# The kv products of six batches: pairs of 128 by 64 column tiles in place of whole-array products of a head pair

## The chip, the cores and the metric

The kernel runs on one core of a Trainium2 chip. The metric is the device time of one execution, in microseconds. Executions of one kernel differ by a few tenths of a per cent, and a change is timed against the kernel before on the same chip.

## The reference

An attention of a linear kind is followed by a two-layer network with a Swish. There are 8 batches, 8 heads, 576 rows and 64 columns per head.

```python
q_s = softmax(q, axis=-1)            # over the 64 columns
k_s = softmax(k, axis=2)             # over the 576 rows
kv  = einsum('bhsd,bhse->bhde', k_s, v)     # 64 x 64 per head: "the kv products"
x   = einsum('bhsd,bhde->bhse', q_s, kv)    # then heads side by side: 4608 x 512
h   = x @ w_in                       # 4608 x 2048
out = (h / (1 + exp(-beta * h))) @ w_out    # 4608 x 512
```

The two large products with `w_in` and `w_out` are most of the arithmetic. The kv products are a small part, and they are what is changed.

## The kernel before

Per batch and head pair, the kernel sums `exp(k)` transposed times `v`. The 576 rows are four slices of 128 and a tail of 64 (padded with zeros to 128), so there are five products per head pair. The values have a column of constants next to them, `D1 = 65` columns per head, so that column 64 gives the softmax denominator.

```python
# batches 2 to 7 (b >= NW); n = 2 head pairs per call
def kv_mm(b, jj, n=2, tag="att"):
    t = ps.tile([P, n, 2 * D1], F32, ...)
    for jl in range(n):
        j = n * jj + jl
        # ... batches 0 and 1: nine products of 65 columns, zero-padded weights ...
        for i in range(R):                     # four slices of 128 rows
            nc.tensor.matmul(
                t[:, jl, :],                                        # 128 x 130
                ek[b][:, i, 2*j : 2*j+2, :].rearrange(...),         # weights 128 x 128: two heads
                va[b][:, i, 2*j : 2*j+2, :].rearrange(...),         # 130 columns: two heads
                start=(i == 0), stop=False)
        nc.tensor.matmul(t[:, jl, :], ekt[...], vt[...], start=False, stop=True)   # the tail
```

Half of each 128 by 130 result is never used: the rows of one head meet the values of the other. `kv_norm` takes the two useful quarters and divides them. The calls are spread among the steps `u` of the large products of the batch before:

```python
def side(c, u):                        # o = 2 for the first batch, else 0
    ...
    if u in (8 + o, 10 + o) and not tail:
        kv_mm(b, (u - 8 - o) // 2)     # "a group": ten products
        kv_norm(b, (u - 8 - o) // 2)
...
for j in range(...):
    mm_a(c, j)          # four 512-column products with w_in
    mm_b(c, j - LAG)    # four 512-column products with w_out
    side(c, j)
```

So each group of ten products stands between 512-column products, and there are 12 groups (two in each of six batches).

The softmax here doesn't subtract the row's maximum and nothing guards it: scores larger than these inputs give would overflow.

Of the kernel before, what the change touches and what calls it, by code (L numbers as in the profile page):

```python
# [10 lines left out]
F32 = mybir.dt.float32  # L11
# [6 lines left out]
def kernel(  # L18
# [10 lines left out]
    nc = tc.nc  # L29
# [6 lines left out]
    NJ = FF // P  # L36
# [5 lines left out]
    NW = 2  # L42
    D1 = D + 1
    LAG = 2
    NCH = B + 1

    const = ctx.enter_context(tc.tile_pool(name="const", bufs=1))
    stage = ctx.enter_context(tc.tile_pool(name="stage", bufs=1))
# [26 lines left out]
    def load_q(b, parts=1):  # L75
        t = stage.tile([P, H, R * D], F32, tag="q_st", bufs=2, name=f"q_st{b}")
        src = q[b, :, 0:MAIN, :].rearrange("h (p i) d -> p h (i d)", i=R)
        n = H // parts
        for s in range(parts):
            nc.sync.dma_start(t[:, s * n : (s + 1) * n, :], src[:, s * n : (s + 1) * n, :])  # L80
        q_st[b] = t
# [12 lines left out]
    def load_kv(d, src, b, tag, parts=1):  # L94
        t = stage.tile([P, H * (R + 1) * D], F32, tag=tag, bufs=2, name=f"{tag}{b}")
        if b < NW:
            d[b] = t[:, 0 : HP * RW * D].rearrange("p (j r) -> p j r", j=HP)
            sv = src[b].rearrange("(j e) (p i) d -> (e p) j (i d)", e=2, i=RW)
            n = HP // parts
            for s in range(parts):  # L100
                nc.sync.dma_start(d[b][:, s * n : (s + 1) * n, :], sv[:, s * n : (s + 1) * n, :])
        else:
            d[b] = t[:].rearrange("p (h r) -> p h r", h=H)
            nc.sync.dma_start(
                d[b][:, :, 0 : R * D], src[b, :, 0:MAIN, :].rearrange("h (p i) d -> p h (i d)", i=R)
            )
            e = b % 2
            nc.sync.dma_start(
                d[b][e * TAIL : (e + 1) * TAIL, :, R * D : R * D + D],
                src[b, :, MAIN:S, :].rearrange("h t d -> t h d"),  # L110
            )
# [140 lines left out]
    def kv_mm(b, jj, n=2, tag="att"):  # L252
        t = ps.tile([P, n, 2 * D1], F32, tag=tag, bufs=2 if tag == "att" else 1, name=f"kv{b}_{jj}")
        att_of[b, jj] = t
        for jl in range(n):
            j = n * jj + jl
            if b < NW:
                for i in range(RW):
                    nc.tensor.matmul(
                        t[:, jl, 0:D1],  # L260
                        ek[b][:, j, i, :],
                        va[b][:, j, i, :],
                        start=(i == 0),
                        stop=(i == RW - 1),
                    )
                continue
            for i in range(R):
                nc.tensor.matmul(
                    t[:, jl, :],
                    ek[b][:, i, 2 * j : 2 * j + 2, :].rearrange("p h d -> p (h d)"),  # L270
                    va[b][:, i, 2 * j : 2 * j + 2, :].rearrange("p h d -> p (h d)"),
                    start=(i == 0),
                    stop=False,
                )
            nc.tensor.matmul(
                t[:, jl, :],
                ekt[(b // 2) % 2][:, ds(j * P, P)],
                vt[(b // 2) % 2][:, b % 2, 2 * j : 2 * j + 2, :].rearrange("p h d -> p (h d)"),
                start=False,
                stop=True,  # L280
            )

    def kv_norm(b, jj, n=2):
        t = att_of.pop((b, jj))
        rk = work.tile([P, n, 1], F32, tag="rk", bufs=2, name=f"rk{b}_{jj}")
        nc.vector.reciprocal(rk[:], t[:, :, D : D + 1])
        for e in range(2):
            r = slice(e * D, (e + 1) * D)
            dst = kvp[r, b, n * jj : n * jj + n, e * D : (e + 1) * D]
            src = t[r, :, 0:D] if b < NW else t[r, :, e * D1 : e * D1 + D]  # L290
            nc.vector.tensor_tensor(dst, src, rk[r].to_broadcast((D, n, D)), ALU.mult)  # L291

    def x_mm(c, j, eng, tag="att"):
# [46 lines left out]
    def mm_b(c, j, sts=range(R)):  # L340
        acc = acc_tiles(c)
        g = g_of[c, j]
        for st in sts:
            nc.tensor.matmul(  # L344
                acc[st][:],
                g[:, ds(st * P, P)],
                w_out_b[:, j, :],
                start=(j == 0),
                stop=(j == NJ - 1),
            )  # L350
# [5 lines left out]
    def store(c, st):  # L356
        acc = acc_of[c]
        eng = nc.scalar if st % 2 == 0 else nc.vector
        if c == B:
            lo, hi = ((0, 2), (0, 2), (2, 3), (3, 4))[st]  # L360
            if st == lo:
                o_of[c] = stage.tile([P, R, DM], F32, tag="wo", bufs=4, name=f"o{c}_{lo}")
            o = o_of[c]
            evac(eng, o[:, st, :], acc[st][:])
            if st == hi - 1:
                for e in range(2):
                    (nc.scalar if st == 2 or (st == 3 and e) else nc.sync).dma_start(
                        out_t[:, MAIN:S, :].rearrange("(i e) t f -> e t i f", e=2)[e, :, lo:hi, :],
                        o[e * TAIL : (e + 1) * TAIL, lo:hi, :],
                    )  # L370
            return
        if st == 0:
            o_of[c] = stage.tile([P, R, DM], F32, tag="wo", bufs=4, name=f"o{c}")
        o = o_of[c]
        evac(eng, o[:, st, :], acc[st][:])
        if st % 2 == 1:
            ov = out[c * S : c * S + MAIN, :].rearrange("(p i) f -> p i f", i=R)
            nc.sync.dma_start(ov[:, st - 1 : st + 1, :], o[:, st - 1 : st + 1, :])
# [41 lines left out]
    ek_buf(1, nc.gpsimd)  # L420
    v_buf(1)

    def load_next(nb):
        if nb < B:
            load_q(nb)
            load_kv(k_st, k, nb, "k_st")
            load_kv(v_st, v, nb, "v_st")
        elif nb == B:
            load_qtail()

    def finish_b(c, j):
        mm_b(c, j)
# [50 lines left out]
    w_cast("in", 1, 1, nc.vector)  # L483
    mm_b(0, 0)
    mm_b(0, 1)
    def pool_cast(*what):
        for kind, blk in what:
            for half in range(2):
                w_cast(kind, blk, half, nc.gpsimd)
# [10 lines left out]
    pool_cast(("in", 3), ("out", 3))  # L500

    for u in range(4, NJ):
        mm_a(0, u)
        mm_b(0, u - LAG)
        if u in (9, 10):
            q_exp(1, u - 9)
        if u in (9, 11):
            q_sum(1, (u - 9) // 2)
        if u in (10, 12):
            q_mul(1, (u - 10) // 2)  # L510
        if u in (11, 13):
            for j in (u - 11, u - 10):
                q_pet(1, j, nc.scalar if u == 11 else nc.vector)
        if u >= 12:
            kz_exp(1, u - 12)
        if u == 14:
            vz_cast(1, 0, nc.vector, m=2)
# [17 lines left out]
    mm_b(1, 0)  # L535
    mm_b(1, 1)

    def side(c, u):
        b = c + 1
        if b > B:  # L540
            return
        tail = b == B
        o = 2 if c == 1 else 0
        if u in (2 + o, 3 + o):
            q_exp(b, u - 2 - o)
            q_sum(b, u - 2 - o)
        if u in (4 + o, 5 + o):
            q_mul(b, u - 4 - o)
            if not tail:
                k_exp(b, u - 4 - o)  # L550
        if u == 4 + o and not tail:
            v_buf(b)
            v_cast(b, nc.gpsimd)
            vtail_cast(b, nc.gpsimd)
        if u == 6 + o:
            if not tail:
                ktail_exp(b)
            q_xbar(b)
        if u in (8 + o, 10 + o) and not tail:
            kv_mm(b, (u - 8 - o) // 2)  # L560
            kv_norm(b, (u - 8 - o) // 2)
        if 11 <= u < 15:
            j = u - 11
            x_mm(b, j, nc.scalar if j % 2 == 0 else nc.vector)
        if u == 9:
            load_next(c + 2)

    for u in range(4):
        side(1, u)
    for c in range(1, NCH):  # L570
        for j in range(4 if c == 1 else 0, NJ - 1 if c == B else NJ):
            lead = c > 1 and j == 3
            if not lead:
                mm_a(c, j)
            if c > 1 and j == 2:
                mm_a(c, 3)
            if (c, j) == (B, NJ - 2):
                pass
            elif j >= LAG:
                mm_b(c, j - LAG)  # L580
            else:
                finish_b(c - 1, NJ + j - LAG)
            side(c, j)
    mm_a(B, NJ - 1, tag="att")
    last = [(0, j) for j in range(NJ - 4, NJ - 1)] + [(1, j) for j in range(NJ - 4, NJ - 1)]
    last += [(0, NJ - 1), (1, NJ - 1)] + [(st, j) for st in (2, 3) for j in range(NJ - 4, NJ)]
    for st, j in last:
        mm_b(B, j, [st])
        if j == NJ - 1:
            store(B, st)  # L590
# [1 line left out]
_INS = ['q', 'k', 'v', 'moe_w_in', 'moe_w_out', 'moe_beta']  # L592
_OUTS = [((4608, 512), 'float32')]
# [25 lines left out]
```

## Time and profile before

| | before |
|---|---|
| median of the first three runs | 293.87 us |
| profiled span | 292.4 us |
| TensorE busy | 279.5 us, 96% |
| one kv group, first start to next matmul | 0.56 us |
| twelve groups | 6.8 us, 2.3% of the span |

First, the line of the profile's first part for the kernel before: busy time, share of the span and count for each engine (PE is TensorE, PEld its weight loads, DVE VectorE, ACT ScalarE).

```profile
PE 279.5 (96%) x1447; PEld 131.0 (45%) x1475; DVE 184.2 (63%) x299; ACT 163.9 (56%) x238; POOL 42.0 (14%) x55
```

The windows view of the same kernel gives the busy time of each engine in a stretch of 28 us in the steady state.

```profile
core 0: us, PE busy (x) PEld busy (x) DVE busy (x) ACT busy (x) POOL busy (x), PEclk, DMA share, GB/s
91.00:119.00 28.00, 27.89 (x143) 13.24 (x144) 17.77 (x31) 16.00 (x24) 2.64 (x3) 1.00 0.62 178
```

TensorE has next to no gap there, at the full clock (1.00), and the other engines are busy for 16 to 18 of 28 us. TensorE sets the pace.

Now the timeline of TensorE around one group. The columns are the start and the recorded length in us, the engine, the line, the operation, the result and operands, the shapes, and how many are merged in the row.

```profile
94.22 0.38 PE L344 MATMUL acc_3_1013<-w_out_b,g_6_1072 128*128 128x512 bf16 x1
94.44 0.39 PE L268 MATMUL kv_0_1107<-va_1046,ek_1044 128*128 128x130 bf16 x4
94.66 0.22 PE L275 MATMUL kv_0_1107<-vt_76,ekt_78 128*128 128x130 bf16 x1
94.72 0.39 PE L268 MATMUL kv_0_1107<-va_1046,ek_1044 128*128 128x130 bf16 x4
94.94 0.22 PE L275 MATMUL kv_0_1107<-vt_76,ekt_78 128*128 128x130 bf16 x1
95.00 0.81 PE L316 MATMUL h_9_1122<-xT_80,w_in_b 128*128 128x512 bf16 x3
```

Read the starts, not the lengths. A 512-column matmul is recorded as 0.38 us long, but the next one starts 0.22 us after it: they are pipelined. The ten products start at 94.44 and the next matmul starts at 95.00, so a product costs 0.056 us. In the trace's own nanoseconds it is 56.7. The weight loads of the same stretch show why nothing stalls at the edges:

```profile
94.22 0.43 PEld L268 LDWEIGHTS <-ek_1044 128*128 128x128 bf16 x4
94.61 0.10 PEld L275 LDWEIGHTS <-ekt_78 128*128 128x128 bf16 x1
```

The first load of the group starts at 94.22, with the 512-column matmul before it, one matmul ahead of its own product (94.44).

Last, the nearest thing to the new products that this kernel has: the 18 products of 65 columns in batch 1, whole array.

```profile
47.23 0.74 PE L259 MATMUL kv_0_612<-va_151,ek_149 128*128 128x65 bf16 x18
47.81 0.38 PE L386 MATMUL warm_635<-kvp 128*128 128x512 bf16 x1
```

From 47.23 to 47.81 is 0.58 us, 32 ns each.

### The profile page before, as it was taken

To read this page: it belongs to the slowest core of one execution; us is meant where nothing else is said; L and a number is where in the kernel's file an instruction comes from. 1 tells how busy PE (TensorE), PEld (TensorE's weight loads), DVE (VectorE), ACT (ScalarE), POOL (GpSimd) and SP (SyncE) were. 2 spreads that over 40 slices of the span, in tenths; PEclk is the share of its full clock that TensorE was granted. 3 is DMA by queue.
4 is the path that set the end of the run, shared out by engine and by line. 5 is a ranking of instruction groups with operands and counts; after the bars stand their busy time and mean duration, and the time that the engine had idled before them with its cause. 6 is when DMAs were issued, how large, how long until landed. Compare 5 with 4: busy or idle time off the path is not lost.

```text
span 292.4 us, 3879 instructions
## 1 busy us (share of the span) xinstructions
PE 279.5 (96%) x1447; PEld 131.0 (45%) x1475; DVE 184.2 (63%) x299; ACT 163.9 (56%) x238; POOL 42.0 (14%) x55
## 2 busy tenths in 40 slices
PE   8898979999999999999999999999999999999991
PEld 3443435445444444454445444544454444544440
DVE  7853696695578557855695469456954694563441
ACT  4863666684486448734773567346825654453340
POOL 4539670300030021002100110003000000000000
PEclk9999999999999999999999999999999999999998
DMA  7999999708932963297319821981293023012005
GB/s 243 378 385 371 377 385 311 248 2 233 296 152 62 315 162 123 62 326 177 123 40 302 223 90 54 303 234 64 84 165 52 32 115 72 0 58 87 0 0 144
DMA packets 55971, 50.06 MB, mean 171 GB/s; under 512 B 26241, under 2 KB 47761, under 8 KB 55953
## 3 DMA queue, kind: packets, MB, share of 16 engines
q1 hardware_dynamic: 55712, 49.43, 55.8%
q10 hardware_dynamic: 240, 0.39, 0.5%
q8 instruction: 11, 0.18, 0.3%
q14 instruction: 8, 0.06, 0.1%
HBM read 36.71 MB, written 9.44 MB: 158 GB/s over the span
## 4 chain that ended last, share of the span: by engine, by line
PE 85%; DMA 6%; DVE 2%; ACT 1%; issue 1%; SPq 1%; another core or an unknown queue 1%; POOL 0%; ACTq 0%
DMA w_out_100<-in_moe_w_out_dram 4%; DMA v_st_91<-in_v_dram 2%; PE acc_3_724 L344 1%; PE acc_2_2458 L344 1%; PE acc_0_2456 L344 1%; PE acc_3_2459 L344 1%; PE acc_1_2167 L344 1%; PE acc_1_1300 L344 1%; PE acc_1_1589 L344 1%; PE acc_1_2728 L344 1%; PE acc_1_1011 L344 1%; PE acc_1_722 L344 1%; PE acc_1_1878 L344 1%; PE acc_2_1879 L344 1%; PE acc_2_1590 L344 1%; PE acc_0_721 L344 1%
## 5 line engine op out<-in xcount | busy, mean ns | idle before, releaser
L316 PEld LDWEIGHTS <-w_in_b 128*128 128x128 bf16 x576 | 55.3, 98 | 65.5 <-issue 2.7
L386 PEld LDWEIGHTS <-kvp 128*128 128x128 bf16 x34 | 3.7, 117 | 6.2 <-issue 3.6
L140 POOL CAST va_2202<-v_st_2007 128x2048 bf16<-128x2048 f32 x1 | 1.9, 1919 | 29.5 <-DMA v_st_2007<-in_v_dram 29.5
L140 POOL CAST va_1913<-v_st_1718 128x2048 bf16<-128x2048 f32 x1 | 1.9, 1918 | 26.7 <-DMA v_st_1718<-in_v_dram 26.7
L140 POOL CAST va_1624<-v_st_1429 128x2048 bf16<-128x2048 f32 x1 | 1.9, 1922 | 26.6 <-DMA v_st_1429<-in_v_dram 26.6
L153 ACT ACTIVATE ek_144<-k_st_86 64x576 bf16<-64x576 f32 x8 | 5.5, 681 | 0.2
L153 ACT ACTIVATE ek_149<-k_st_118 64x576 bf16<-64x576 f32 x8 | 5.4, 676 | 0.0
L140 POOL CAST va_1046<-v_st_836 128x2048 bf16<-128x2048 f32 x1 | 1.9, 1920 | 24.0 <-DMA v_st_836<-in_v_dram 24.0
L140 POOL CAST va_1335<-v_st_1140 128x2048 bf16<-128x2048 f32 x1 | 1.9, 1917 | 22.7 <-DMA v_st_1140<-in_v_dram 22.7
L296 PEld LDWEIGHTS <-kvp 128*128 128x128 bf16 x32 | 3.1, 98 | 4.2 <-DVE kvp L291 1.0
L140 POOL CAST va_147<-v_st_91 128x576 bf16<-128x576 f32 x4 | 3.3, 860 | 6.3 <-DMA v_st_91<-in_v_dram 6.3
L209 ACT ACTIVATE eq_189<-q_st_83 128x1024 bf16<-128x1024 f32 x2 | 2.1, 1056 | 3.0 <-DMA q_st_83<-in_q_dram 3.0
L140 POOL CAST va_783<-v_st_132 128x2048 bf16<-128x2048 f32 x1 | 1.9, 1916 | 12.2 <-DMA v_st_132<-in_v_dram 12.2
L140 POOL CAST w_in_b<-w_in_114 128x1024 bf16<-128x1024 f32 x2 | 3.0, 1536 | 2.1 <-DMA w_in_114<-in_moe_w_in_dram 2.1
L226 DVE TENSOR_TENSOR eq_485<-eq_485,rq_487 128x1024 bf16<-128x1024 bf16 x2 | 3.3, 1652 | 0.0
L140 POOL CAST w_out_b<-w_out_100 128x1024 bf16<-128x1024 f32 x2 | 2.4, 1205 | 4.6 <-DMA w_out_100<-in_moe_w_out_dram 4.6
L140 POOL CAST w_out_b<-w_out_116 128x1024 bf16<-128x1024 f32 x2 | 2.6, 1292 | 1.7 <-DMA w_out_116<-in_moe_w_out_dram 1.7
L220 DVE TENSOR_REDUCE rq_191<-eq_189 128x16 f32<-128x1024 bf16 x2 | 2.4, 1215 | 0.3 <-ACT eq_189 L209 0.3
L220 DVE TENSOR_REDUCE rq_487<-eq_485 128x16 f32<-128x1024 bf16 x2 | 2.4, 1212 | 0.3 <-ACT eq_485 L209 0.3
L220 DVE TENSOR_REDUCE rq_748<-eq_746 128x16 f32<-128x1024 bf16 x2 | 2.4, 1212 | 0.3 <-ACT eq_746 L209 0.3
L220 DVE TENSOR_REDUCE rq_1887<-eq_1885 128x16 f32<-128x1024 bf16 x2 | 2.4, 1191 | 0.3 <-ACT eq_1885 L209 0.3
L220 DVE TENSOR_REDUCE rq_2176<-eq_2174 128x16 f32<-128x1024 bf16 x2 | 2.4, 1190 | 0.3 <-ACT eq_2174 L209 0.3
(1461 smaller groups left out, 838.9 us busy)
## 6 DMA issues: line engine op xcount, KB each, us to landing
k_st_86<-in_k_dram SPq DMA_DIRECT2D x4, 288.0 KB, 5.7
v_st_91<-in_v_dram SPq DMA_DIRECT2D x4, 288.0 KB, 6.5
k_st_118<-in_k_dram SPq DMA_DIRECT2D x4, 288.0 KB, 9.6
v_st_124<-in_v_dram SPq DMA_DIRECT2D x2, 576.0 KB, 9.3
q_st_83<-in_q_dram SPq DMA_DIRECT2D x2, 512.0 KB, 4.3
w_in_97<-in_moe_w_in_dram SPq DMA_DIRECT2D x2, 512.0 KB, 6.4
w_out_100<-in_moe_w_out_dram SPq DMA_DIRECT2D x2, 512.0 KB, 9.3
w_in_102<-in_moe_w_in_dram SPq DMA_DIRECT2D x1, 1024.0 KB, 9.3
```

What stands on the lines that cost most here:

```text
L140: eng.tensor_copy(dst, src)
L153: nc.scalar.activation(ek[b][r, j : j + m, :, e * D : (e + 1) * D], k_st[b][r, j : j + m, :].rearrange("p j (i d) -> p j i d", i=RW), ACTF ...
L209: nc.scalar.activation(eq[b][:, :, s * m : (s + 1) * m, :].rearrange("p i h d -> p h i d"), q_st[b][:, s * m : (s + 1) * m, :].rearrange(" ...
L220: nc.vector.tensor_reduce(rq[b][:, 0, :, h], eq[b][:, :, h, :], axis=AX.X, op=ALU.add)
L226: nc.vector.tensor_tensor(eq[b][:, :, h, :], eq[b][:, :, h, :], rq[b][:, 1, :, h].unsqueeze(3).to_broadcast((P, R, m, D)), ALU.mult,)
L296: nc.tensor.matmul(t[:], kvp[:, c, j, :], qsT[c][:, :, j, :])
L316: nc.tensor.matmul(h[:], w_in_b[:, kt, ds(j * P, P)], x_of(c)[:, kt, :], start=(kt == 0), stop=(kt == KT - 1),)
L344: nc.tensor.matmul(acc[st][:], g[:, ds(st * P, P)], w_out_b[:, j, :], start=(j == 0), stop=(j == NJ - 1),)
L386: nc.tensor.matmul(t[:, 0:cols], kvp[:, B - 1, 0, :], kvp[:, B - 1, :, :].rearrange("p j r -> p (j r)")[:, 0:cols],)
```

## The change

The intent is to stop computing the unused half. The array is used as two tiles of 128 rows by 64 columns. Each head's product goes to its own tile and streams only its own 65 columns. If the two tiles work side by side, a pair of products takes the time of one 65-column product.

```diff
+    FIX, LASTMAIN, COLT = False, False, True
 ...
     def kv_mm(b, jj, n=2, tag="att"):
 ...
+            if COLT:
+                for i in range(R + 1):
+                    for e in range(2):
+                        hd = 2 * j + e
+                        nc.tensor.matmul(
+                            t[e * D : (e + 1) * D, jl, 0:D1],
+                            ek[b][:, i, hd, :] if i < R else ekt[(b // 2) % 2][:, ds(hd * D, D)],
+                            va[b][:, i, hd, :] if i < R else vt[(b // 2) % 2][:, b % 2, hd, :],
+                            start=(i == 0),
+                            stop=(i == R),
+                            tile_position=(0, e * D),
+                        )
+                continue
 ...
     def kv_norm(b, jj, n=2):
 ...
-            src = t[r, :, 0:D] if b < NW else t[r, :, e * D1 : e * D1 + D]
+            src = t[r, :, 0:D] if b < NW or COLT else t[r, :, e * D1 : e * D1 + D]
```

The rest of the diff (cut here) adds two switches, `FIX` and `LASTMAIN`, which are off, and rewrites the loop so that it can be reordered; with the switches off the order is the same. Comparing the instruction streams shows that only the kv products and their loads differ (120 products become 240), and the place that one of the two multiplies in each `kv_norm` reads.

More of the change, by code (lines that the diff above doesn't have):

```diff
@@ L44 @@
     LAG = 2
+    FIX, LASTMAIN, COLT = False, False, True
     NCH = B + 1
+    order = list(range(NCH))
+    if LASTMAIN:
+        order[B - 1], order[B] = B, B - 1
+    LASTC = order[-1]
     const = ctx.enter_context(tc.tile_pool(name="const", bufs=1))
@@ L358, in store @@
         eng = nc.scalar if st % 2 == 0 else nc.vector
+        if c == B and c != LASTC:
+            if st == 0:
+                o_of[c] = stage.tile([P, R, DM], F32, tag="wo", bufs=4, name=f"o{c}")
+            o = o_of[c]
+            evac(eng, o[:, st, :], acc[st][:])
+            if st % 2 == 1:
+                for e in range(2):
+                    nc.sync.dma_start(
+                        out_t[:, MAIN:S, :].rearrange("(i e) t f -> e t i f", e=2)[e, :, st - 1 : st + 1, :],
+                        o[e * TAIL : (e + 1) * TAIL, st - 1 : st + 1, :],
+                    )
+            return
         if c == B:
@@ L366, in store @@
                 for e in range(2):
-                    (nc.scalar if st == 2 or (st == 3 and e) else nc.sync).dma_start(
+                    if FIX:
+                        q_eng = (nc.sync, nc.sync, nc.gpsimd, nc.scalar if e else nc.sync)[st]
+                    else:
+                        q_eng = nc.scalar if st == 2 or (st == 3 and e) else nc.sync
+                    q_eng.dma_start(
                         out_t[:, MAIN:S, :].rearrange("(i e) t f -> e t i f", e=2)[e, :, lo:hi, :],
@@ L370, in store @@
                     )
+            return
+        if c == LASTC:
+            o = stage.tile([P, R, DM], F32, tag="wo", bufs=4, name=f"o{c}_{st}")
+            evac(eng, o[:, st, :], acc[st][:])
+            ov = out[c * S : c * S + MAIN, :].rearrange("(p i) f -> p i f", i=R)
+            (nc.sync, nc.scalar, nc.sync, nc.sync)[st].dma_start(ov[:, st, :], o[:, st, :])
             return
@@ L421, with load_next @@
     v_buf(1)
-    def load_next(nb):
-        if nb < B:
-            load_q(nb)
-            load_kv(k_st, k, nb, "k_st")
-            load_kv(v_st, v, nb, "v_st")
-        elif nb == B:
+    def load_next(n):
+        if order[n] < B:
+            load_q(order[n])
+        else:
             load_qtail()
+        if n < B:
+            load_kv(k_st, k, n, "k_st")
+            load_kv(v_st, v, n, "v_st")
     def finish_b(c, j):
@@ L502 @@
     for u in range(4, NJ):
-        mm_a(0, u)
+        if not (FIX and u == 5):
+            mm_a(0, u)
+        if FIX and u == 4:
+            mm_a(0, 5)
+            mm_b(0, 2)
+            continue
+        if FIX and u in (12, 14):
+            for j in (u - 12, u - 11):
+                q_pet(1, j, nc.scalar if u == 12 else nc.vector)
         mm_b(0, u - LAG)
@@ L510 @@
             q_mul(1, (u - 10) // 2)
-        if u in (11, 13):
+        if not FIX and u in (11, 13):
             for j in (u - 11, u - 10):
@@ L536, with side @@
     mm_b(1, 1)
-    def side(c, u):
-        b = c + 1
-        if b > B:
+    def side(n, u):
+        if n + 1 >= NCH:
             return
-        tail = b == B
-        o = 2 if c == 1 else 0
+        qc = order[n + 1]
+        kb = n + 1
+        o = 2 if n == 1 else 0
         if u in (2 + o, 3 + o):
-            q_exp(b, u - 2 - o)
-            q_sum(b, u - 2 - o)
+            q_exp(qc, u - 2 - o)
+            q_sum(qc, u - 2 - o)
         if u in (4 + o, 5 + o):
-            q_mul(b, u - 4 - o)
-            if not tail:
-                k_exp(b, u - 4 - o)
-        if u == 4 + o and not tail:
-            v_buf(b)
-            v_cast(b, nc.gpsimd)
-            vtail_cast(b, nc.gpsimd)
-        if u == 6 + o:
-            if not tail:
-                ktail_exp(b)
-            q_xbar(b)
-        if u in (8 + o, 10 + o) and not tail:
-            kv_mm(b, (u - 8 - o) // 2)
-            kv_norm(b, (u - 8 - o) // 2)
+            q_mul(qc, u - 4 - o)
+            if kb < B:
+                k_exp(kb, u - 4 - o)
+        if u == 4 + o and kb < B:
+            v_buf(kb)
+            v_cast(kb, nc.gpsimd)
+            vtail_cast(kb, nc.gpsimd)
+        if u == 6 + o:
+            if kb < B:
+                ktail_exp(kb)
+            q_xbar(qc)
+        if u in (8 + o, 10 + o) and kb < B:
+            kv_mm(kb, (u - 8 - o) // 2)
+            kv_norm(kb, (u - 8 - o) // 2)
         if 11 <= u < 15:
             j = u - 11
-            x_mm(b, j, nc.scalar if j % 2 == 0 else nc.vector)
-        if u == 9:
-            load_next(c + 2)
+            x_mm(qc, j, nc.scalar if j % 2 == 0 else nc.vector)
+        if u == 9 and n + 2 < NCH:
+            load_next(n + 2)
     for u in range(4):
         side(1, u)
-    for c in range(1, NCH):
-        for j in range(4 if c == 1 else 0, NJ - 1 if c == B else NJ):
-            lead = c > 1 and j == 3
-            if not lead:
+    for n in range(1, NCH):
+        c = order[n]
+        for j in range(4 if n == 1 else 0, NJ - 1 if n == B else NJ):
+            if not (n > 1 and j == 3):
                 mm_a(c, j)
-            if c > 1 and j == 2:
+            if n > 1 and j == 2:
                 mm_a(c, 3)
-            if (c, j) == (B, NJ - 2):
+            if (n, j) == (B, NJ - 2):
                 pass
@@ L581 @@
             else:
-                finish_b(c - 1, NJ + j - LAG)
-            side(c, j)
-    mm_a(B, NJ - 1, tag="att")
+                finish_b(order[n - 1], NJ + j - LAG)
+            side(n, j)
+    mm_a(LASTC, NJ - 1, tag="att")
     last = [(0, j) for j in range(NJ - 4, NJ - 1)] + [(1, j) for j in range(NJ - 4, NJ - 1)]
@@ L587 @@
     for st, j in last:
-        mm_b(B, j, [st])
+        mm_b(LASTC, j, [st])
         if j == NJ - 1:
-            store(B, st)
+            store(LASTC, st)
 _INS = ['q', 'k', 'v', 'moe_w_in', 'moe_w_out', 'moe_beta']
```

## The prediction

> **What bounds the kernel now.** TensorE: the busy table gives it 279.5 of 292.4 us (96%), the chain of waits is 85% TensorE. In the steady state no other engine holds it up: between 91 and 119 us it is busy 27.9 of 28.0 us at clock 1.00, VectorE 17.8, ScalarE 16.0. A nanosecond saved on TensorE there reaches the end almost whole. The diff's other switches are off: the order of instructions is the same on every engine except inside the kv products.
>
> **What the products cost.** Batches 2 to 7 issue two groups each of ten 130-column products with 128x128 weight loads. In the timeline one group runs from 94.44 to 95.00 us, where the next matmul starts: 56 ns each; the loads are hidden, and the 512-column neighbours keep their 215 ns spacing. Twelve groups: 6.8 us, 2.3% of the span.
>
> **What the change does.** 120 products of 130 columns become 240 of 65, in pairs for two halves of the array, with 240 loads of 64 columns.  Three terms, all on the critical path:
>
> 1. *Streaming.* If a pair runs side by side at the price of one 65-column product (about 30 ns, an estimate: half of 56 plus a little), 120 x 26 = 3.1 us are saved. If serial, the nearest in the trace is batch 1: eighteen 65-column products in 0.58 us, 32 ns each, so a pair is 64 ns: 1.0 us lost.
> 2. *Weight loads.* The Trainium skill, TensorEngine Tiling, Restrictions, says column tiling disables Fast Weight Load; no run here shows it yet. Slower loads, twice as many, may set the pace: 35 to 50 ns each (a guess) is 70 to 100 ns a pair, 1.7 to 5.3 us lost.
> 3. *Switches.* The same page, Key Properties, says that changing the tiling mode drains TensorE; not shown here either. A group sits between 512-column matmuls: 24 switches. Such a matmul lasts 380 ns and the next starts after 215 ns, so a drain exposes up to 165 ns, and a load (98 ns) may no longer hide: at worst 24 x 0.26 = 6.3 us, at best near nothing. I take 0.12 us each, 2.9 us.
>
> Sum: I expect -0.7 us from terms 1 and 2 together (the gain only partly had) and +2.9 us from term 3: +2.2 us.
>
> **Predicted time: 296.0 us, range 292.2 to 301.0.** Faster by over 2%: 0.01 (the kv work is only 2.3%). Within 2%: 0.84. Slower by over 2%: 0.15.
>
> **What will show each step.**
> - Streaming: the two products of a pair start a few ns apart and pairs follow at about 30 ns (side by side), or all start 27 to 35 ns apart (serial), or further (loads set the pace).
> - Loads: how long a 64-column load lasts, against 98 ns, and whether its starts set the products' spacing.
> - Switches: the gap from the last 512-column start to the first kv start, 216 ns now, and from the last kv start to the next matmul, 56 ns now. A drain shows as 300 ns or more before, 150 ns or more after.
> - Group length, 0.56 us now: 0.5 to 0.6 us for the products alone, and about 0.25 us of switching around them.
>
> **What would make it wrong.** Tiles that overlap, loads included, with free switches: 291 us. Serial slow loads with full drains on both sides: 303 us or more. The start (before 50 us) I take to be the same to 0.5 us.

## The result, and the profile after

| | before | after |
|---|---|---|
| median, first comparison (6 runs each) | 294.14 us | 293.75 us |
| ratio of the means, 95% interval | | 0.9989 (0.9964 to 1.0013) |
| profiled span | 292.4 us | 291.4 us |
| steady part (defined below) | 237.108 us | 236.845 us |

A ratio in this document is the mean time of one kernel's runs over that of the other's runs of the same rounds, so it is not quite the ratio of the medians quoted. Executions over 1.5% slower than the fastest of the same kernel are left out of the means.

The change is inside the noise of the timed runs. A finer measure helps. In each profile I took the time from the start of the last 65-column product of batch 1 to the start of the last matmul of the kernel, from the trace's start times in nanoseconds. I call it the steady part. The stretch before it is loading and start-up, and it came out between 47.5 and 48.8 us in the twelve profiles, in no relation to the change; that spread alone is several times the effect. The steady part is far calmer: 236.845 and 236.846 us in two profiles of the changed kernel.

The same lines of the kernel after, first the busy line and the same window:

```profile
PE 279.2 (96%) x1565; PEld 128.2 (44%) x1595; DVE 184.4 (63%) x299; ACT 163.8 (56%) x238; POOL 40.9 (14%) x55
```

```profile
91.00:119.00 28.00, 27.84 (x163) 12.73 (x164) 17.64 (x31) 16.14 (x23) 2.65 (x3) 1.00 0.61 178
```

By these nothing happened: TensorE is as busy as before. The timeline of TensorE around the same group says otherwise.

```profile
93.49 0.38 PE L362 MATMUL acc_3_1033<-w_out_b,g_6_1092 128*128 128x512 bf16 x1
93.80 0.32 PE L276 MATMUL kv_0_1127<-va_1066,ek_1064 128*64 128x65 bf16 x8
93.95 0.20 PE L276 MATMUL kv_0_1127<-vt_76,ekt_78 128*64 128x65 bf16 x2
93.98 0.29 PE L276 MATMUL kv_0_1127<-va_1066,ek_1064 128*64 128x65 bf16 x8
94.11 0.20 PE L276 MATMUL kv_0_1127<-vt_76,ekt_78 128*64 128x65 bf16 x2
94.24 1.04 PE L334 MATMUL h_9_1152<-xT_80,w_in_b 128*128 128x512 bf16 x3
```

Two things changed, in opposite directions. The twenty products run from 93.80 to 94.11 us, where the ten ran from 94.44 to 94.94. But the step from the last 512-column matmul to the group is 0.31 us, where it was 0.22, and from the last product to the next matmul it is 0.13 us, where it was 0.06. The recorded 0.38 us of the 512-column matmul (93.49 to 93.87) covers the new gap entirely, which is why the busy share cannot show it.

The weight loads of the same stretch:

```profile
93.80 0.20 PEld L276 LDWEIGHTS <-ek_1064 128*64 128x64 bf16 x8 [0.42 <-ACT th_8_1119 L344]
93.92 0.12 PEld L276 LDWEIGHTS <-ekt_78 128*64 128x64 bf16 x2
93.95 0.21 PEld L276 LDWEIGHTS <-ek_1064 128*64 128x64 bf16 x8
94.08 0.11 PEld L276 LDWEIGHTS <-ekt_78 128*64 128x64 bf16 x2
94.23 0.55 PEld L334 LDWEIGHTS <-w_in_b 128*128 128x128 bf16 x4
```

The first load of the group no longer starts one matmul ahead. It starts at 93.80, with its own product; the first load after the group starts at 94.23, with its own matmul at 94.24. The bracket says that the loads sat idle for 0.42 us until ScalarE finished `th_8`. Releasers are inferred, and this one I came to doubt; the view of that line lists what the waits before its loads were put down to in all:

```profile
its engine sat idle before it (us, times) until:
  issue: 2.5, 6
  ACT th_10_844 L344: 0.4, 1
  ACT th_8_1428 L344: 0.4, 1
  ACT th_8_1737 L344: 0.4, 1
  ACT th_8_2046 L344: 0.4, 1
  ACT th_8_1119 L344: 0.4, 1
  ACT th_8_2355 L344: 0.4, 1
```

Half of the twelve waits have a ScalarE instruction beside them and half have none, while the gap itself, in nanoseconds, is 309 or 310 at nine of the twelve groups (525 at the other three, where one 512-column record is missing from the trace).

In nanoseconds, a mean group gives this ledger (from the last 512-column start before it to the second matmul start after it; stretches with a missing record are left out). The first step is called the lead-in below.

| step | before | after | difference |
|---|---|---|---|
| last 512-column start to first kv start | 216 | 309 | +93 |
| first kv start to last kv start | 510 | 312 | -198 |
| last kv start to next matmul start | 57 | 129 | +72 |
| that matmul to the one after it | 216 | 226 | +10 |
| sum | 999 | 976 | -23 |

Twelve groups give -0.28 us, and the steady part changed by -0.263 us. The ledger closes.

Split by cause: the products of a pair start 3 to 7 ns apart, and pairs follow each other at 31.9 ns where single products followed at 56.7, so ten pairs save 10 x 24.8 = 248 ns. Against this stand 93 ns before the first pair, 20 ns before the second pair (52 ns in place of 32), 100 ns after the last pair and 10 ns after the next matmul: 223 to 224 ns. I call this sum the cost of an excursion into the column-tile mode: 12 x 0.224 = 2.69 us paid, 12 x 0.248 = 2.97 us saved.

The trace also tells where in an edge the time passes. On entry the first load starts 307 or 308 ns after the last 512-column start, and its product follows 1 or 2 ns later; on exit the first load starts 124 to 126 ns after the last kv start, and its product follows 4 or 5 ns later. So nearly all of the 93 and the 100 ns pass before the first load of the new kind begins. In both cases that load begins 71 to 73 ns before the recorded end of the last product of the old kind.

### The profile page after: what moved, and what is told of

Same layout as the page of the kernel before. It is cut to its first block, busy times and chain, and to the rows that moved or that the text cites. A ratio compares the mean times of both kernels' runs of the same rounds, so it can differ in the third digit from the quotient of the medians.

```text
span 291.4 us, 4117 instructions
## 1 busy us (share of the span) xinstructions
PE 279.2 (96%) x1565; PEld 128.2 (44%) x1595; DVE 184.4 (63%) x299; ACT 163.8 (56%) x238; POOL 40.9 (14%) x55
## 4 chain that ended last, share of the span: by engine, by line
PE 83%; DMA 8%; DVE 3%; ACT 2%; issue 1%; POOL 1%; SPq 0%; ACTq 0%; POOLq 0%
DMA w_in_114<-in_moe_w_in_dram 4%; DMA w_in_97<-in_moe_w_in_dram 2%; DMA k_st_86<-in_k_dram 2%; PE acc_2_2578 L362 1%; PE acc_0_2576 L362 1%; PE acc_0_1957 L362 1%; PE acc_3_1033 L362 1%; PE acc_1_722 L362 1%; PE acc_3_1960 L362 1%; PE acc_1_1649 L362 1%; PE acc_2_2849 L362 1%; PE acc_1_1958 L362 1%; PE acc_2_723 L362 1%; PE acc_0_1648 L362 1%; PE acc_0_1030 L362 1%; PE acc_3_724 L362 1%
## 5 line engine op out<-in xcount | busy, mean ns | idle before, releaser
L145 DVE CAST w_in_b<-w_in_102 128x1024 bf16<-128x1024 f32 x2 | 3.6, 1790 | 0.0
L145 POOL CAST w_out_b<-w_out_100 128x1024 bf16<-128x1024 f32 x2 | 2.1, 1040 | 4.2 <-DMA w_out_100<-in_moe_w_out_dram 4.2
L225 DVE TENSOR_REDUCE rq_191<-eq_189 128x16 f32<-128x1024 bf16 x2 | 2.4, 1216 | 0.3 <-ACT eq_189 L214 0.3
L225 DVE TENSOR_REDUCE rq_487<-eq_485 128x16 f32<-128x1024 bf16 x2 | 2.4, 1218 | 0.3 <-ACT eq_485 L214 0.3
L225 DVE TENSOR_REDUCE rq_748<-eq_746 128x16 f32<-128x1024 bf16 x2 | 2.4, 1214 | 0.3 <-ACT eq_746 L214 0.3
L225 DVE TENSOR_REDUCE rq_1040<-eq_1038 128x16 f32<-128x1024 bf16 x2 | 2.4, 1192 | 0.3 <-ACT eq_1038 L214 0.3
L225 DVE TENSOR_REDUCE rq_2276<-eq_2274 128x16 f32<-128x1024 bf16 x2 | 2.4, 1190 | 0.3 <-ACT eq_2274 L214 0.3
L225 DVE TENSOR_REDUCE rq_1658<-eq_1656 128x16 f32<-128x1024 bf16 x2 | 2.4, 1190 | 0.3 <-ACT eq_1656 L214 0.3
```

The source lines that it names most:

```text
L145: eng.tensor_copy(dst, src)
L225: nc.vector.tensor_reduce(rq[b][:, 0, :, h], eq[b][:, :, h, :], axis=AX.X, op=ALU.add)
```

## The experiments

Theory A: the pairs run side by side, the whole saving is had, and entering and leaving the column-tile mode takes almost all of it back. The rivals: B, the kv products are not what bounds the kernel, so neither term reaches the end; C, the gap before a group is a wait for ScalarE, as the profile has it; D, it matters where the groups stand; E, small products are cheap by themselves and the two tiles have nothing to do with it; F, the gap comes from the change of the kind of weight load, not of the mode.

The results together; the steady part is from one profile of each, the ratio to the kernel before on the same chip. No kernel differs from before by as much as 2%; what is told apart here is one per cent and less.

| kernel | steady part, us | against before | median, us | ratio (95%) |
|---|---|---|---|---|
| before | 237.108 | | | |
| after_again | 236.846 | -0.26 | 293.52 | 0.9992 (0.9972 to 1.0012) |
| adj_col | 235.485 | -1.62 | 292.44 | 0.9948 (0.9930 to 0.9966) |
| adj_full | 237.118 | +0.01 | 294.00 | 1.0004 (0.9986 to 1.0022) |
| split_col | 239.528 | +2.42 | 295.47 | 1.0055 (1.0040 to 1.0070) |
| split_full | 237.072 | -0.04 | 294.10, one run | |
| serial | 239.443 | +2.34 | 295.98 | 1.0072 (1.0048 to 1.0096) |
| excursion | 240.206 | +3.10 | 296.70 | 1.0098 (1.0071 to 1.0124) |
| merged4 | 235.475 | -1.63 | 292.06 | 0.9944 (0.9913 to 0.9976) |
| load127 | 237.305 | +0.20 | 294.06, one run | |
| wide | 239.829 | +2.72 | 295.87, one run | |

The first four after "before" (after_again to split_col) ran on one chip, where before had a median of 293.93 us (11 runs); split_full to merged4 on another, 294.09 us (11 runs); the last two on a third, 294.68 us (one run). The three single runs are of unknown state and are read by spacings inside the trace and by the steady part.

### after_again: the change with more rounds

No edit.

> The changed kernel again, with more rounds, to size the small difference. Ledger from the trace of the first run: a group of ten pairs takes 32 ns a pair in place of 57 ns a product (-2.97 us over 12 groups), and entering and leaving the column-tile mode adds about 224 ns per group (+2.69 us over 12). Theory A (gain had in full, eaten by the switches): net -0.29 us, ratio 0.999 to before. Rival B (the kv products are not what TensorE is bound by, so neither term reaches the end): ratio 1.000.

The ratio is 0.9992 with an interval that includes 1, so the timed runs cannot tell A from B. The steady part repeats to 1 ns.

### adj_col: half as many excursions

```diff
-        if u in (8 + o, 10 + o) and kb < B:
-            kv_mm(kb, (u - 8 - o) // 2)
-            kv_norm(kb, (u - 8 - o) // 2)
+        if u == 8 + o and kb < B:
+            kv_mm(kb, 0)
+            kv_mm(kb, 1)
+            kv_norm(kb, 0)
+            kv_norm(kb, 1)
```

> The changed kernel with the two groups of a batch issued one right after the other (at the place of the first), so the mode is entered and left 6 times in place of 12. The products are the same. Theory A (switches cost 224 ns per entry and exit together): 6 x 0.224 = 1.34 us less than the changed kernel, 1.63 us less than before, ratio 0.9944, about 292.4 us. Rival B (not bound there): no change, 0.999. Rival C (the 93 ns before a group are a wait for ScalarE, which the profile names as releaser before some groups, not a switch): the second group of the batch loses its lead-in only by chance; I would see the gap kept, and less than 0.5 us gained.

The steady part fell by 1.36 us against the change, where 1.34 was expected, and by 1.62 against before, where 1.63 was expected. The ratio, 0.9948, is where A put it (0.9944). The timeline of TensorE shows that the second group of a batch has no lead-in of its own:

```profile
93.70 0.20 PE L276 MATMUL kv<-vt,ekt 128*64 128x65 bf16 x2
93.74 0.29 PE L276 MATMUL kv<-va,ek 128*64 128x65 bf16 x8
93.86 0.20 PE L276 MATMUL kv<-vt,ekt 128*64 128x65 bf16 x2
93.89 0.29 PE L276 MATMUL kv<-va,ek 128*64 128x65 bf16 x8
...
94.31 1.04 PE L334 MATMUL h<-xT,w_in_b 128*128 128x512 bf16 x4
```

The second group starts at 93.89, 0.03 us after the last row of the first at 93.86. Rival B is out: TensorE time removed here reaches the end in full.

### adj_full: the same move without column tiles

The same edit on the kernel before.

> Control: the kernel before with the same move of the second group, no column tiles. Theory A: nothing to save, since no mode changes: ratio 1.000 within 0.001. If moving the group itself is worth something (rival D: the gain of the adjacent version comes from the place, not from the switches), this run is as much faster as the adjacent column-tiled one: ratio 0.995.

Ratio 1.0004, steady part +0.01 us. The move by itself is worth nothing, so rival D is out for this move.

### split_col: twice as many excursions

```diff
-        if u in (8 + o, 10 + o) and kb < B:
-            kv_mm(kb, (u - 8 - o) // 2)
-            kv_norm(kb, (u - 8 - o) // 2)
+        if 7 + o <= u < 11 + o and kb < B:
+            kv_mm(kb, u - 7 - o, n=1)
+            kv_norm(kb, u - 7 - o, n=1)
```

> The changed kernel with each batch's products in four groups of five pairs, 512-column matmuls between them: 24 entries and exits in place of 12. Theory A: 12 x 0.224 = 2.69 us more than the changed kernel, 2.4 us more than before, ratio 1.008, about 296.4 us. Rival B: 0.999. VectorE has 24 more small instructions in all batches together, which should not matter since it is 63% busy.

The steady part is 2.42 us over before, exactly the 2.4 expected. All 24 groups have a lead-in of 309 or 310 ns. With 6, 12 and 24 excursions and the same products, the steady part is 235.485, 236.846 and 239.528 us: 0.227 us per excursion between the first two, 0.223 between the last two.

The timed runs show less: a ratio of 1.0055, which is 1.6 us over before in place of 2.4, and the upper end of the interval (1.0070, 2.1 us) does not reach 2.4. Part of it lies outside the kernel's own span. Each timed run lists its span too: before, the timed value is 2.15 us above the span in the mean, and here 1.79. By the spans alone split_col is 1.98 us over before (293.75 against 291.77). The remaining 0.4 us is within what the start-up varies by, but the timed runs have no timeline to show it, and why the part outside the span is shorter here is open too (column tiles are not needed for it: the one run of split_full, below, has 1.80).

### split_full: the control for it

The same edit on the kernel before.

> Control for the split version: the kernel before with its products in four groups of five, no column tiles. Theory A: no mode to change, so the steady part stays 237.1 us within 0.1. Rival D (places matter): up to 2.7 us longer.

The steady part is 237.072 us, within 0.04 us of before. Four groups instead of two cost nothing when no mode changes.

### serial: the same tiles, not side by side

```diff
-                for i in range(R + 1):
-                    for e in range(2):
-                        hd = 2 * j + e
-                        nc.tensor.matmul(...)          # tiles alternate
+                for e in range(2):                     # all of tile 0, then all of tile 1
+                    for jl in range(n):
+                        hd = 2 * (n * jj + jl) + e
+                        for i in range(R + 1):
+                            nc.tensor.matmul(...)
```

> The changed kernel with the same 20 products per group in another order: all ten of the first column tile, then all ten of the second, so that neighbours never use different tiles (but once). Loads, switches, results are the same. Theory A (the gain is the two tiles running side by side): about 30 to 32 ns per product, 600 ns per group in place of 312, so 12 x 0.29 = 3.5 us more than the changed kernel, steady part 236.85 + 3.5 = 240.3 us, total about 297.1, ratio 1.011. Rival E (a 65-column product with a 64-column load is simply cheap by itself, 16 ns, and what the order is does not matter): no change, steady part 236.85 us, ratio 0.999.

The steady part rose by 2.60 us against the change, not by 3.5. The direction is A's and rival E is out: in this order a product of 65 columns costs 29 to 36 ns. The size was off because the two tiles' work overlapped at the change from one tile to the other. (Loop control is cut from the diff.) In the timeline of TensorE the middle of a group stands out:

```profile
94.92 0.31 PE L279 MATMUL kv<-va,ek 128*64 128x65 bf16 x4
95.07 0.20 PE L279 MATMUL kv<-vt,ekt 128*64 128x65 bf16 x1
95.10 0.32 PE L279 MATMUL kv<-va,ek 128*64 128x65 bf16 x7
95.23 0.20 PE L279 MATMUL kv<-vt,ekt 128*64 128x65 bf16 x1
95.26 0.20 PE L279 MATMUL kv<-va,ek 128*64 128x65 bf16 x1
```

The first row has four products in 0.15 us; the third has seven in 0.13. After its first tail product (95.07) the first tile has only four `va` products left before its second tail product (95.23), so three of the seven belong to the second tile: they were issued later and started earlier. In nanoseconds, three starts in this stretch come 1, 6 and 7 ns after another. So three of the twenty products were hidden behind others, and the group took about 527 ns.

### excursion: the mode change alone

The kernel before, untouched but for a dummy pair of column-tile products after each group. The pair writes spare columns of the same result tile; results stay right. (The result tile becomes one head pair wider, and `kv_norm` reads the first `n` only.)

```diff
+        if b >= NW:
+            for e in range(2):
+                nc.tensor.matmul(
+                    t[e * D : (e + 1) * D, n, 0:D1],      # spare columns
+                    ek[b][:, 0, e, :], va[b][:, 0, e, :],
+                    start=True, stop=True, tile_position=(0, e * D))
```

> The kernel before, its 130-column products untouched, with one dummy pair of 65-column column-tile products after each of the 12 groups (into spare columns, on operands that the group has just used, so with no new wait): the switch alone. Theory A: entry about 150 ns after the last 130-column product's start in place of 57, pair to next matmul 129, next spacing 226: +235 ns per group, 12 x 0.235 = 2.8 us, steady part 237.11 + 2.8 = 239.9 us, total about 296.7, ratio 1.010. If the cost of the changed kernel's edges were a wait of its operands for ScalarE (rival C), only the pair's own 30 ns each would be added: 0.4 us, ratio 1.001. It also tells whether the cost depends on the length of the product before the switch (130 columns here, 512 before).

The steady part rose by 3.10 us, 258 ns per group. I had expected 235: in the sum I had taken 129 ns from the pair to the next matmul and forgotten that the first pair in the mode takes about 20 ns longer. Less the pair itself (32 ns) it is 226 ns, the excursion's cost from the ledger (224). The timeline of TensorE:

```profile
94.14 0.22 PE L276 MATMUL kv<-vt,ekt 128*128 128x130 bf16 x1
94.29 0.22 PE L285 MATMUL kv<-va,ek 128*64 128x65 bf16 x2
94.44 1.04 PE L327 MATMUL h<-xT,w_in_b 128*128 128x512 bf16 x4
```

The pair's operands had been in use for 0.6 us, so it has nothing to wait for, and yet it starts 0.15 us after the 130-column product, not 0.057. Rival C is out: the ScalarE instruction named beside the gap was a neighbour in time. The lead-in is 94 ns longer than usual after a 130-column product and 93 ns after a 512-column one, so it does not grow with the product before it. The exits agree: here, after a lone pair, the first load starts 146 or 147 ns after the last product's start, and again 71 or 72 ns before its recorded end.

### merged4: the candidate

```diff
-        if u in (8 + o, 10 + o) and kb < B:
-            kv_mm(kb, (u - 8 - o) // 2)
-            kv_norm(kb, (u - 8 - o) // 2)
+        if u == 8 + o and kb < B:
+            kv_mm(kb, 0, n=4)
+            kv_norm(kb, 0, n=4)
 ...
-        t = ps.tile([P, n, 2 * D1], F32, ...)
+        t = ps.tile([P, n, D1 if COLT and b >= NW else 2 * D1], F32, ...)
```

> The candidate: one group of four head pairs per batch[...], one reciprocal and two multiplies per batch in place of two and four. Theory A: TensorE as in the adjacent version, steady part 235.49 us, total 292.4, ratio 0.9945; VectorE is not on the critical path, so its fewer instructions give nothing more.

Median 292.06 us, ratio 0.9944, steady part 235.475 us, results right: 0.6% better than before, and 10 ns from the adjacent version in the steady part. One result tile serves all four head pairs, since each now takes 65 columns of it in place of 130. The smaller number of VectorE instructions gave nothing more, as expected. Of the mean gain, 0.35 us lies outside the span, as in split_col (1.80 us above it, where before has 2.15); by spans the gain is 1.29 us, and 1.56 us in the adjacent version. One of its six runs took 294.62 us, which widens the interval.

### load127: another kind of load, the same mode

Its output is wrong, which doesn't matter for the time. The whole array stays in use, but four of five loads have 127 columns.

```diff
             for i in range(R):
                 nc.tensor.matmul(
-                    t[:, jl, :],
-                    ek[b][:, i, 2 * j : 2 * j + 2, :].rearrange("p h d -> p (h d)"),
+                    t[0 : P - 1, jl, :],
+                    ek[b][:, i, 2 * j : 2 * j + 2, :].rearrange("p h d -> p (h d)")[:, 0 : P - 1],
 ...
-                start=False,        # the tail product
+                start=True,
```

> Wrong result on purpose: the kernel before, whole array, but with weight loads of 127 columns in place of 128 for four of the five products of each head pair (the fifth, 128 wide, starts the sum anew, so only the tail rows count). It tells the mode from the load: if the 93 ns before a group and about 100 after it come from changing the column-tile mode (theory A), a load that is merely of the slower kind changes nothing at the edges: lead-in 216 ns, group to next matmul 57 ns. If they come from changing between the fast and the plain kind of weight load (rival F), the lead-in is about 309 ns and every group shows two or more such stalls, since the fifth product goes back to 128 columns. What a plain load of 127 columns does to the pace inside a group is open: 57 ns if it still hides, more if not.

In the trace's operands, a 128-column load reads its weights as four runs of 32, and both the 127-column and the 64-column loads read theirs as one run: the plain kind. The loads of 127 columns are recorded at 137 to 140 ns against 98. The timeline of TensorE:

```profile
93.84 0.40 PE L268 MATMUL kv<-va,ek 128*127 128x130 bf16 x4
94.07 0.22 PE L275 MATMUL kv<-vt,ekt 128*128 128x130 bf16 x1
94.13 0.40 PE L268 MATMUL kv<-va,ek 128*127 128x130 bf16 x4
94.36 0.22 PE L275 MATMUL kv<-vt,ekt 128*128 128x130 bf16 x1
94.42 0.81 PE L316 MATMUL h<-xT,w_in_b 128*128 128x512 bf16 x3
```

From the last product to the next matmul is 0.06 us, and the lead-in is 215 or 216 ns at each group. There is no stall when the kind of load changes, inside the group or at its edges, so rival F is out. Inside the group a product takes 59 ns in place of 57, which is all that a plain 127-column load costs here (+0.20 us in the steady part).

### wide: the mode without fewer columns

```diff
-                            t[e * D : (e + 1) * D, jl, 0:D1],
+                            t[e * D : (e + 1) * D, jl, :],
 ...
-                            va[b][:, i, hd, :] if i < R else vt[...][:, b % 2, hd, :],
+                            (va[b][:, i, 2*j : 2*j+2, :] if i < R else vt[...][:, b % 2, 2*j : 2*j+2, :]).rearrange(...),
```

> The changed kernel with each tile streaming both heads' 130 columns (half of each result unused, as before the change); results right. Same loads, same tiles, same switches, double the columns. If a pair's 32 ns is set by streaming its 65 columns, a pair now takes about 57 ns, as one whole-array product did, and the kernel is the one before plus the switches alone: steady part 237.11 + 2.7 = 239.8 us. If the 32 ns is set by the two loads or by issue with room to spare in streaming, a pair takes less than 57 ns; if the tiles contend while streaming, more.

(`kv_norm` reads as in the kernel before.) Steady part 239.829 us, 239.8 expected. The timeline of TensorE:

```profile
93.64 0.42 PE L276 MATMUL kv<-va,ek 128*64 128x130 bf16 x8
93.89 0.22 PE L276 MATMUL kv<-vt,ekt 128*64 128x130 bf16 x2
93.95 0.39 PE L276 MATMUL kv<-va,ek 128*64 128x130 bf16 x8
```

A pair takes 57 ns, as one whole-array product of 130 columns did; each tile streams its 130 columns and the other tile does not disturb it. This is the kernel before plus twelve excursions (2.72 us), nothing else. Since the loads are the same as in the change, they do not set the 57 ns; the pace follows the columns. Nor do they show in the 32 ns of the change: in batch 1 a 65-column product on the whole array, with 128-column loads, takes 32 ns too.

## Why the prediction was right or wrong

It was right that TensorE bounds the steady state and that time there reaches the end in full: 6, 12 and 24 excursions moved the steady part as the ledger said. It was right that the kv products, 6.8 us, are all that the change can touch, and that the result would be within 2%.

**Term 3, the switches, was right in place and size.** The prediction took 0.12 us for each of 24 switches, 2.9 us, out of a range that went from near nothing to 0.26; that it came so near is partly luck. The runs show 0.112 each, 2.69 us, and they show it three ways (the ledger, the count of excursions, the lone excursion). The mode change itself is what the Trainium skill states (TensorEngine Tiling, Key Properties: "Mode switching requires drain"); this trace agrees, in that every change of the mode has a stall, and adds the number. The expected shape was wrong in part: a drain was to show as up to 165 ns from the recorded length of a 512-column matmul, but the first load starts 72 ns before that recorded end (93.80 against 93.87 us), and 93 ns is what is lost. After a group, 150 ns or more was named as the sign of a drain; the gap was 129.

**The step that failed is the sum of terms 1 and 2: "I expect -0.7 us from terms 1 and 2 together (the gain only partly had)".** They came to -2.97 us. Term 1, in its side-by-side form, was right: pairs follow at 31.9 ns where 30 was assumed, so 3.0 us is saved where 3.1 was assumed. What failed is term 2, the slower loads, which the prediction guessed at 35 to 50 ns each in series, 70 to 100 ns a pair and 1.7 to 5.3 us lost; at most 2 ns a pair over the assumed 30, some 0.2 us, can be theirs. The prediction's own sign says the same: 0.5 to 0.6 us was named for the products of a group, and they took 0.31. The Trainium skill (TensorEngine Tiling, Restrictions) says that column tiling goes without Fast Weight Load. The trace fits that: the 64-column loads are of the plain kind and are recorded at 106 to 114 ns, longer than the 98 ns of a 128-column load. It doesn't show that the tiling is the reason, since the 127-column loads of load127 are plain on the whole array. But the 64-column loads are not taken in series. Loads for the two tiles start about 3 ns apart, overlap with the products of both tiles, and a pair still follows at 32 ns. The same skill's page on the engine (TensorE: Matmul & The Clock Gate, Part 3) gives about 4 ns between the starts of concurrent tiles, and the trace agrees with 3 to 7, mostly 3 or 4.

So a forecast of +2.2 us met a result of -0.3 us (-0.263 in the steady part), because a guess about loads had been mixed with a sound figure for streaming. The nearest measured evidence was there to be read: with whole-array loads, batch 1's products kept 32 ns apiece, with each load hidden. In these runs the length of a load record said little about the pace that it allowed.

What stays open is what TensorE does in the 93 ns and the 100 ns of an entry and an exit. The runs show that they do not depend on the length of the product before, on semaphores or on the kind of load. The first load's recorded time is not in them, for it begins at their end. At 183 entries and exits of the eight profiles with column tiles (9 more lack a record) it begins 71 to 73 ns before the recorded end of the product before it, whether that is 379, 220, 218 or 193 to 198 ns long. As times from start to start this is 308 ns after 512 columns, 148 after 130 and 125 after 65: each some 92 ns more than the usual spacing of such products (216, 57 and 32). A fixed time for emptying the array would look like that, in both directions; but the recorded ends are the profiler's reckoning and the array itself is not seen, so this is argued and not shown. Nor is it shown why split_col's timed runs gained back some 0.8 us, of which 0.36 lies outside the span.

## What to carry to other kernels

In this kernel column tiles gave their whole gain inside a group, but entering and leaving the mode cost 0.22 us together, nine times the 25 ns that one pair saves; so a group here needs more than nine pairs to break even, ten pairs here gained 0.02 us, and twenty pairs gained 0.27. Put all tiled products of a stretch next to each other before judging the mode. When two terms of opposite sign are near in size, predict each by the smallest thing measured and look in the timeline at starts, not at busy shares: here the busy share hid both terms.

## What the Trainium skill lacked or had wrong

- TensorEngine Tiling (Array Packing), Key Properties, says that changing the mode drains TensorE but gives no cost. Here an entry costs 93 to 94 ns plus 20 ns before the second pair, after 512 columns as after 130, and an exit 100 ns plus 10 ns: 224 ns for both. The first load of the new kind starts some 92 ns later than the next product of the old kind would have.
- The same page, Restrictions, lists the loss of Fast Weight Load and does not say what it costs. Here plain 64-column loads of two tiles (106 to 114 ns as recorded) hid behind pairs at 31.9 ns, and plain 127-column loads (137 to 140 ns) raised the pace of 130-column products only from 57 to 59 ns.
- TensorE: Matmul & The Clock Gate, Part 3, says, in its list of what overlaps, that weight loads overlap with running matmuls only where the row groups differ (its text above that list also names the background weight buffer). Here both tiles use all 128 rows and the loads still overlapped: pairs at 31.9 ns with two loads of over 100 ns each between them.
- The same part of that page says that matmuls start in strict program order. In the serial run, by the recorded starts, three products of the second tile started before the last product of the first tile, which stands ahead of them in the program.
- The same page, LDWEIGHTS, gives the time of a load as its columns over 1.2 (an estimate by that rule: 53 ns for 64). Here the records are 106 to 114 ns for 64 columns and 137 to 140 ns for 127, plain; neither is the pace.
